# Stores one tile behind, weight transposes held back, and a split first and last tile in a fused attention and FFN training kernel

## The chip, the cores and the metric

The kernel runs on one core of a Trainium2 chip. The metric is the device time of one execution in microseconds; before the change the median of four runs was 837.86 us (839.8, 839.36, 836.18, 836.36). Engine names follow the profile: PE is TensorE, PEld its weight loads, DVE VectorE, ACT ScalarE, POOL GpSimd and SP SyncE. SP does nothing but issue transfers; ACT and POOL issue some as well, and a "queue" is the list of transfers that one engine issues in order.

## What is computed

The reference is the forward pass and all the gradients of one transformer block, with S = 2048 rows, width D = 640, FFN width F = 1728, 32 heads of 20, in bf16:

```python
def _A_ref(x, wqkv, wo):                       # linear attention
    q, k, v = split_heads(x @ wqkv)            # 32 heads x 20
    phi = lambda t: jnp.where(t > 0, t + 1, jnp.exp(t)) + 1e-6
    pq, pk = phi(q), phi(k)
    kv  = einsum("bhsd,bhse->bhde", pk, v)
    z   = einsum("bhsd->bhd", pk)
    num = einsum("bhqd,bhde->bhqe", pq, kv)
    den = einsum("bhqd,bhd->bhq", pq, z)[..., None] + 1e-6
    return merge_heads(num / den) @ wo
def _B_ref(x, w_gate, w_up, w_down):
    return (silu(x @ w_gate) * (x @ w_up)) @ w_down

h  = x + _A_ref(layernorm(x), wqkv, wo)
h2 = h + _B_ref(layernorm(h), w_gate, w_up, w_down)
outputs: h2, and for a given grad_out the gradients of x, wqkv, wo, w_gate, w_up, w_down
```

## The kernel before

The 2048 rows are 16 row tiles of 128 (ST = 16); 640 columns are five blocks of 128 (DT = 5) and, for the accumulators in PSUM, two halves of 320 columns (NCH); F is 14 blocks of 128, the last one not full (FT = 14). One matmul therefore is mostly 128 x 128 weights by 320 columns. `mm_row` (its matmul is line 118) writes both halves of one accumulator. Accumulators come from a pool of four, row tiles of work from pools of five and later seven (`wk`), big tensors from a pool of five (`big`), strips from a pool of four.

The stages, in the order of time, with the rows of before.py:

- *Layer norm 1 and the projections* (8 to 58 us, lines 181 to 288). `load_x` brings row tiles of x, `wqk` holds the k and q columns of wqkv, loaded in a K half (line 186) and a Q half (line 188), all on SP's queue except tile 1, which ACT issues. `ln1_stats(t)` takes mean and variance (lines 124, 125) and from them rstd (129, 130); for the first two tiles a part of this is on DVE and the last step on POOL. `ln1(t)` normalises into xn (line 238, DVE), transposes five blocks on PE (242), and copies them out on ACT as xnT (243). `kq_mm(t, 0)` and `kq_mm(t, 1)` are the two projections, with phi on ACT (251, 252) and DVE (257, 259). In this part the program order on PE, DVE and ACT is the written order: stats of tile 0, stats of tile 1, xn of tile 0, and so on.
- *z, Y, KVT and the normalisation* (58 to about 100 us). The sum of phi(k) over the rows is formed as zs and zl (297, 298) and spread as zb (386). `KVT`, one half of the strip `yk`, is filled with zeros (379) before masked blocks are written into it (400). `normalise` divides the phi(q) tiles (366 to 373). W2 is KVT by wo.
- *h1 and layer norm 2* (100 to about 152 us, lines 413 to 438). At tile t the residual is added (422) and stored; two tiles behind (u = t - 2) hn is formed (437). In five of these steps a block of W2 is transposed by SP into a `stg` buffer and written by POOL to the DRAM scratch scr_W2T (435). rstd of this layer norm runs on POOL too.
- *FFN forward and backward in four column groups* (152 to 460 us), ending in scratch copies: the columns needed for dhn, and the w_down gradient transposed, scr_dwdT.
- *The dh1 loop* (460 to 614 us, lines 592 to 638). At tile t, PE computes dhn from `cols` (54 matmuls a tile), `ln_bwd` ends in dh (143), SP transposes it into dh1T (603). Three tiles behind (LAG_C = 3, u = t - 3) PE multiplies dh1T by W2T into ps_dp, and DVE forms dq through pr, S1 and nS1. Besides, POOL loads the row tile pqr (606), DVE multiplies it into pqs_tm (623), and for the first 14 tiles SP transposes one block of the w_down gradient, dwd (609), which POOL stores to the output (611). Before the last tile's dp, three blocks of GT = dh1^T pqs_tm are accumulated over the first 15 row tiles (`gt_part`, 587), and their last row tile comes after.
- *GT, dKVT, dz and WV2* (614 to 631 us, lines 645 to 703). SP transposes wqkv in 15 pieces into wqkvT (`tr_mat`, `tr_piece`, 566). ACT issues the load of all x rows again as xn_r (`act_load`, 148), which DVE normalises (690). GT and dKVT are stored to scratch by POOL (667, 677). WV2 is copied by ACT (699) and transposed by SP as wvk (700).
- *The wqkv gradient and dxn* (630 to 765 us): per row tile, SP transposes pk, dq and dk into a ring of tiles (717, 718, 750), and PE multiplies them by wqkvT and wvk (767). xnT is read back in four parts by ACT.
- *The output* (765 to 834 us, lines 805 to 826): per row tile 28 matmuls of the FFN's activations by w_down (815), the add of h1 (818), a store by POOL (819). The last tile has its two halves in two accumulators, with an add (822) and a store (823) for each, by ACT and by SP.

What sets the order: `tc.manual_schedule(engines=...)` keeps the written order on the engines named; in the dh1 loop and after only on SP (then SP and DVE). On the others a scheduler orders the program by its own estimate of when operands are ready, so that a line that stands later can be issued earlier. `tc.issue_after(i)` puts what it encloses behind the instruction i on the same engine; it adds no wait. A written order holds inside its block: the 15 transposes of wqkvT stand in the code behind the whole dh1 loop, in the next block, and yet twelve of them are issued on SP between the transposes dh1T of the last two tiles.

Of the kernel before, what the change touches and what calls it, by code (L numbers as in the profile page):

```python
# [10 lines left out]
ALU = mybir.AluOpType  # L11
# [4 lines left out]
P = 128  # L16
# [4 lines left out]
def kernel(  # L21
# [161 lines left out]

    load_x(nc.sync, 0, 1)
    load_x(nc.scalar, 1, 2)
    nc.sync.dma_start(out=wqk[:, :, D:2 * D], in_=A_wqkv[:, D:2 * D].rearrange("(k p) n -> p k n", p=P))
# [50 lines left out]
    def ln1(t):  # L237
        nc.vector.tensor_scalar(out=xn[:, t, :], in0=x_tm[t // 8][:, t % 8, :], scalar1=mv1[:, t, 0:1],
                                scalar2=rstd1[:, t:t + 1], op0=ALU.subtract, op1=ALU.mult)
        tp = psum.tile([P, D], BF16, name="ps_t", tag="mm")  # L240
        for kt in range(DT):
            nc.tensor.transpose(tp[:, kt * P:(kt + 1) * P], xn[:, t, kt * P:(kt + 1) * P], ident[:])
        nc.scalar.copy(out=xnT[:, t], in_=tp[:].rearrange("p (k c) -> p k c", c=P))  # L243

# [21 lines left out]
    with tc.manual_schedule(engines={EngineType.PE, EngineType.DVE, EngineType.Activation}):  # L266
# [4 lines left out]
        ln1_stats(0)  # L271
        ln1_stats(1)
        ln1(0)
# [101 lines left out]
    with tc.manual_schedule(engines={EngineType.PE, EngineType.DVE}):  # L375
        yk = strips.tile([P, 2, DT, D], BF16, name="yk", tag="S")
        Yt = yk[:, 0]
        KVT = yk[:, 1]
        nc.vector.memset(KVT, 0.0)
        for i in range(DT):  # L380
# [35 lines left out]
        for t in range(ST + 2):  # L416
# [151 lines left out]

    def tr_mat(dst, src):
        for i in range(DT):  # L570
            tr_piece(dst, src, i)

    with tc.manual_schedule(engines={EngineType.SP}):
# [4 lines left out]
        pqs_tm = big.tile([P, ST, D], BF16, name="pqs_tm", tag="B")  # L578
        pqr = {}
        dh1Ts = {}  # L580

# [10 lines left out]
        for t in range(ST + LAG_C):  # L592
            if t < ST:
                if t % 2 == 0 and 2 < t + 2 < ST:
                    load_cols(t // 2 + 1)
                cols = colp[t // 2]
                ps = mm("ps_dhn")
                mm_row(ps, lambda k: cols[:, t % 2, k, :],
# [3 lines left out]
                dh1Ts[t] = dh1T[:].rearrange("p (k c) -> p k c", c=P)  # L602
                nc.sync.dma_start_transpose(out=dh1Ts[t], in_=dh1[:, t, :])
# [19 lines left out]
            nc.vector.tensor_tensor(out=hb(pqs_tm[:, u, :]), in0=hb(pq[:]), in1=bc(rall[:, u, :]), op=ALU.mult)  # L623
            dp = wk("dp")
# [15 lines left out]
    with tc.manual_schedule(engines={EngineType.SP, EngineType.DVE}):  # L640
# [13 lines left out]
        for k in (2, 0, 1):  # L654
            tr_mat(wqkvT[:, 5 * k:5 * k + 5, :], A_wqkv[:, k * D:(k + 1) * D])
        act_load(xn_r[:], x_v)

        GT = mat("GT")
        for i in range(DT):
            ps = gts.pop(i, None)  # L660
            if ps is None:
                ps = mm("ps_gt")
                gt_part(ps, i, 0, ST)
            else:
                gt_part(ps, i, ST - 1, ST)
            nc.scalar.copy(out=half(GT[:, i, :]), in_=row(ps))
# [138 lines left out]
        for t in range(ST):  # L805
# [5 lines left out]
            ps = mm("ps_o")  # L811
            pss = [ps, ps] if t < ST - 1 else [ps, mm("ps_o2")]
            for ci, (n0, n1) in enumerate(NCH):
                for j in range(FT):
                    nc.tensor.matmul(pss[ci][:, ci, :320], lhsT=mT[:, t % 4, j, :], rhs=wd[:, j, n0:n1],  # L815
                                     start=(j == 0), stop=(j == FT - 1))
            if t < ST - 1:
                nc.vector.tensor_tensor(out=half(h1r[:]), in0=row(ps), in1=half(h1r[:]), op=ALU.add)  # L818
                nc.gpsimd.dma_start(out=o0_v[:, t, :], in_=h1r[:])
            else:  # L820
                for ci, (n0, n1) in enumerate(NCH):
                    nc.vector.tensor_tensor(out=h1r[:, n0:n1], in0=pss[ci][:, ci, :320], in1=h1r[:, n0:n1], op=ALU.add)
                    (nc.scalar, nc.sync)[ci].dma_start(out=o0_v[:, t, n0:n1], in_=h1r[:, n0:n1])
            if t < DT:
# [34 lines left out]
```

## Time and profile before

One execution was profiled; every number below is of that one.

| | us |
|---|---|
| time of the profiled execution | 839.06 |
| its span (first to last instruction) | 837.1 |
| median of four runs | 837.86 |
| PE busy | 825.4 (99%) |
| DVE busy | 444.0 (53%) |
| ACT busy | 291.6 (35%) |
| POOL busy | 190.2 (23%) |
| granted clock of PE, mean | 0.998 |

A row of a timeline has the start, the duration, the engine, the line in before.py, the operation and its operands as out<-in, how many equal instructions the row holds (x10), and in brackets the idle time of the engine before it and what ended it. A row "SPq" or "ACTq" is the issuing of transfers, not the transfers. A row of the waits says which engine waited at which line for which engine or transfer: total us, times, longest. "Landing" is the time from the start of the issue to the arrival of the data. Row tiles are counted from 0, so the last is tile 15.

### The profile page before, as it was taken

The page shows a single profiled execution, that of the slowest core. Times are in us where ns is not written, and L with a number is a line of the kernel's source. Part 1 is how long each engine was busy: PE and PEld are TensorE (multiplying, and loading weights), DVE is VectorE, ACT ScalarE, POOL GpSimd, SP SyncE. Part 2 cuts the span into 40 slices and gives each one's busy share as a digit, 9 for nine tenths or more (in the row PEclk, how much of TensorE's full clock was granted, in tenths as well). Part 3 has the DMA queues.
Part 4 walks back from the last instruction along what each step waited for, and adds up shares of the span by engine and source line. Part 5 has one row for each costly group of instructions (what it writes and reads, how often), then busy time and mean ns, then how long its engine had stood idle before and what let it go on. Part 6 is the DMA issues. An engine that isn't in the chain of part 4 may idle for free.

```text
span 837.1 us, 13990 instructions
## 1 busy us (share of the span) xinstructions
PE 825.4 (99%) x5509; PEld 528.3 (63%) x5509; DVE 444.0 (53%) x872; ACT 291.6 (35%) x414; POOL 190.2 (23%) x347
## 2 busy tenths in 40 slices
PE   8999999999999999999999999999999999999998
PEld 6666656555555555555656777777666677777776
DVE  7979757791086028700940155797854266621121
ACT  6983422770184035401920232322222133331101
POOL 2330133222412312231225012111101122111322
PEclk9999999999999999999999999999999999999999
DMA  9995889998668988992686769656579988899962
GB/s 295 207 328 137 170 164 251 261 220 208 160 138 215 209 185 187 208 231 70 148 236 172 249 172 246 168 113 153 115 216 224 152 145 176 165 199 215 271 181 95
DMA packets 282785, 160.17 MB, mean 191 GB/s; under 512 B 238128, under 2 KB 269408, under 8 KB 282720
## 3 DMA queue, kind: packets, MB, share of 16 engines
q1 hardware_dynamic: 253472, 80.71, 51.0%
q0 software_dynamic: 17968, 65.55, 25.4%
q10 hardware_dynamic: 11280, 13.03, 5.8%
q8 instruction: 43, 0.70, 0.4%
q14 instruction: 22, 0.18, 0.1%
HBM read 47.43 MB, written 55.10 MB: 122 GB/s over the span
## 4 chain that ended last, share of the span: by engine, by line
PE 87%; DVE 6%; DMA 3%; SPq 2%; ACT 1%; issue 1%; POOL 0%; DVEq 0%; ACTq 0%; POOLq 0%
PE ps_dw L533 20%; PE ps_dhn L118 14%; PE ps_dxn L767 8%; PE ps_o L815 7%; PE pg L465 6%; PE pu L470 5%; PE ps_dwqk L118 5%; PE ps_dm L309 4%; PE ps_kq L118 3%; PE ps_y L118 3%; PE ps_dk L118 2%; PE ps_dp L118 2%; PE pdm L309 2%; PE ps_a L118 2%; PE ps_gt L587 1%; DMA ring<-dk 1%
## 5 line engine op out<-in xcount | busy, mean ns | idle before, releaser
L118 PE MATMUL ps_dhn<-wgT,cols 128*128 128x320 bf16 x864 | 119.5, 299 | 0.0
L533 PE MATMUL ps_dw<-dd,hn 128*128 128x448 bf16 (+1 forms) x640 | 118.8, 346 | 0.0
L118 PEld LDWEIGHTS <-cols 128*128 128x128 bf16 x864 | 84.5, 98 | 32.9
L533 PEld LDWEIGHTS <-hn 128*128 128x128 bf16 x640 | 62.6, 98 | 54.2
L535 DVE CAST dwev<-ps_dw 128x896 bf16<-128x896 f32 (+3 forms) x12 | 10.9, 908 | 124.1 <-PE ps_dw L533 124.1
L502 POOL DMA_DIRECT2D scr_dT<-stg x64 | 34.7, 543 | 168.6 <-DMA stg<-dd 166.1
L535 ACT CAST dwev<-ps_dw 128x896 bf16<-128x896 f32 (+1 forms) x20 | 17.6, 879 | 158.0 <-PE ps_dw L533 158.0
L465 PE MATMUL pg<-wgu,hnT 128*128 128x448 bf16 (+1 forms) x320 | 63.6, 346 | 0.0
L470 PE MATMUL pu<-wgu,hnT 128*128 128x448 bf16 (+1 forms) x320 | 63.6, 346 | 0.0
L815 PE MATMUL ps_o<-wd,mT 128*128 128x320 bf16 x448 | 62.6, 299 | 0.0
L767 PEld LDWEIGHTS <-ring 128*128 128x128 bf16 x480 | 47.5, 99 | 21.5 <-DMA ring<-dk 2.3
L533 PE MATMUL ps_dw<-m_s,dh 128*128 128x448 bf16 (+1 forms) x320 | 60.5, 346 | 0.3 <-DVE m_s L497 0.3
L815 PEld LDWEIGHTS <-mT 128*128 128x128 bf16 x448 | 43.8, 98 | 17.0
L767 PE MATMUL ps_dxn<-wqkvT,ring 128*128 128x320 bf16 x320 | 52.6, 304 | 2.0 <-DMA ring<-dk 2.0
L533 PEld LDWEIGHTS <-dh 128*128 128x128 bf16 x320 | 31.3, 98 | 27.5 <-issue 0.5
L470 PEld LDWEIGHTS <-hnT 128*128 128x128 bf16 x320 | 31.3, 98 | 27.1
L465 PEld LDWEIGHTS <-hnT 128*128 128x128 bf16 x320 | 31.3, 98 | 27.1
L309 PEld LDWEIGHTS <-dh2T 128*128 128x128 bf16 x320 | 31.3, 98 | 25.1
L118 PE MATMUL ps_kq<-wqk,xnT 128*128 128x320 bf16 x320 | 46.1, 299 | 0.8 <-ACT xnT L243 0.8
L309 PE MATMUL ps_dm<-wdT,dh2T 128*128 128x448 bf16 (+1 forms) x240 | 46.9, 344 | 0.0
L818 DVE TENSOR_TENSOR h1r<-ps_o,h1r 128x640 bf16<-128x640 f32 x15 | 12.4, 825 | 56.6 <-PE ps_o L815 36.8
L118 PEld LDWEIGHTS <-xn_r 128*128 128x128 bf16 x320 | 30.7, 98 | 13.4 <-DVE xn_r L690 1.6
(159 smaller groups left out, 1288.3 us busy)
## 6 DMA issues: line engine op xcount, KB each, us to landing
cols<-scr_dT POOLq DMA_DIRECT2D x7, 1728.0 KB, 8.5
scr_dT<-stg POOLq DMA_DIRECT2D x48, 224.0 KB, 3.2
scr_m<-m_s POOLq DMA_DIRECT2D x12, 448.0 KB, 5.0
out_dram<-dwev POOLq DMA_DIRECT2D x30, 112.0 KB, 2.1
scr_dT<-stg POOLq DMA_DIRECT2D x16, 192.0 KB, 3.2
scr_xnT<-xnT SPq DMA_DIRECT2D x4, 640.0 KB, 6.0
scr_pk<-pk SPq DMA_DIRECT2D x4, 640.0 KB, 6.7
scr_pq<-pqa SPq DMA_DIRECT2D x4, 640.0 KB, 7.9
```

The lines of the kernel that those rows point to most:

```text
L118: nc.tensor.matmul(ps[:, ci, :320], lhsT=lhs(k), rhs=rhs(k, n0, n1), start=(start and k == 0), stop=(stop and k == n - 1))
L309: nc.tensor.matmul(ps[:, c, :w], lhsT=dh2T[:, kt, (t + c) * P:(t + c + 1) * P], rhs=wdT[:, kt, o:o + w], start=(kt == 0), stop=(kt == DT - 1))
L465: nc.tensor.matmul(pg[:, c, :w], lhsT=hnT[:, kt, (t + c) * P:(t + c + 1) * P], rhs=wg[:, kt, 0:w], start=(kt == 0), stop=(kt == DT - 1))
L470: nc.tensor.matmul(pu[:, c, :w], lhsT=hnT[:, kt, (t + c) * P:(t + c + 1) * P], rhs=wg[:, kt, w:2 * w], start=(kt == 0), stop=(kt == DT - 1))
L502: nc.gpsimd.dma_start(out=scr_dT[t + c, :, KO[g]:KO[g] + GK[g], :], in_=stg[:, :GK[g], :])
L533: nc.tensor.matmul(ps[:, c, :w], lhsT=lhs(t), rhs=rhs(t), start=(t == 0), stop=(t == ST - 1))
L535: copy(out=ev[:, :len(parts), :w], in_=ps[:, :len(parts), :w])
L587: nc.tensor.matmul(ps[:, ci, :320], lhsT=dh1[:, t, i * P:(i + 1) * P], rhs=pqs_tm[:, t, n0:n1], start=(t == 0), stop=(t == ST - 1))
L767: nc.tensor.matmul(ps[:, ci, :320], lhsT=lhs[:, i, :], rhs=rhs[:, i, n0:n1], start=(k == 0 and i == 0), stop=(k == 2 and i == DT - 1))
L815: nc.tensor.matmul(pss[ci][:, ci, :320], lhsT=mT[:, t % 4, j, :], rhs=wd[:, j, n0:n1], start=(j == 0), stop=(j == FT - 1))
L818: nc.vector.tensor_tensor(out=half(h1r[:]), in0=row(ps), in1=half(h1r[:]), op=ALU.add)
```

## The change

- The load of x tile 0 is split in two halves of 320 columns, one by SP and one by ACT; tile 1 moves from ACT to SP, behind the first half. The statistics of tile 1 move from before xn of tile 0 to behind it. The copy of the first xnT is shared: blocks 0 to 2 by ACT, blocks 3 and 4 by DVE.
- The fill of KVT with zeros is put behind the subtraction that makes zl, on DVE. (In the program before, the scheduled place was in the middle of layer norm 1, at 26.84 us.)
- The store of a W2T block is written one tile later than its transpose.
- The transpose of a w_down gradient block goes ahead of the tile's dh1T on SP, and its store one tile later. The multiply into pqs_tm goes one tile earlier, right behind the load of pqr.
- The 15 transposes of wqkvT are put behind the last dh1T. The three parts of GT before the last dp stop two row tiles earlier (13 instead of 15 row tiles); the two tiles come after.
- The last output tile is computed in pieces of 320, 192 and 128 columns, each with its own add and store, by ACT, POOL and SP.

```diff
-    load_x(nc.sync, 0, 1)
-    load_x(nc.scalar, 1, 2)
+    nc.sync.dma_start(out=x_tm[0][:, 0, 0:320], in_=x_v[:, 0, 0:320])
+    nc.scalar.dma_start(out=x_tm[0][:, 0, 320:640], in_=x_v[:, 0, 320:640])
+    load_x(nc.sync, 1, 2)
...
-        nc.scalar.copy(out=xnT[:, t], in_=tp[:].rearrange("p (k c) -> p k c", c=P))
+        tpv = tp[:].rearrange("p (k c) -> p k c", c=P)
+        if t == 0:
+            ln1_stats(1)
+            nc.scalar.copy(out=xnT[:, t, 0:3], in_=tpv[:, 0:3])
+            nc.vector.tensor_copy(out=xnT[:, t, 3:5], in_=tpv[:, 3:5])
+        else:
+            nc.scalar.copy(out=xnT[:, t], in_=tpv)
...
         ln1_stats(0)
-        ln1_stats(1)
         ln1(0)
...
-        nc.vector.tensor_tensor(out=half(zs[1][:]), in0=row(ps), in1=half(zs[0][:]), op=ALU.subtract)
+        last_zs = nc.vector.tensor_tensor(out=half(zs[1][:]), in0=row(ps), in1=half(zs[0][:]), op=ALU.subtract).ins
...
-        nc.vector.memset(KVT, 0.0)
+        with tc.issue_after(last_zs):
+            nc.vector.memset(KVT, 0.0)
...
+            if 2 <= u <= DT + 1:
+                nc.gpsimd.dma_start(out=mat_v(scr_W2T)[:, :, (u - 2) * P:(u - 1) * P], in_=w2t)
             if 1 <= u <= DT:
                 w2t = stage()[:, :DT, :]
                 nc.sync.dma_start_transpose(out=w2t, in_=W2[:, u - 1, :])
-                nc.gpsimd.dma_start(out=mat_v(scr_W2T)[:, :, (u - 1) * P:u * P], in_=w2t)
...
+                if t < FT:
+                    dwds[t] = wk("dwd", pool=1)
+                    nc.sync.dma_start_transpose(out=dwds[t][:].unsqueeze(1), in_=scr_dwdT[:, t * P:(t + 1) * P])
...
-                nc.sync.dma_start_transpose(out=dh1Ts[t], in_=dh1[:, t, :])
-            if t - LAG_C + 1 in range(ST):
-                pqr[t - LAG_C + 1] = wk("pqr", pool=1)
-                nc.gpsimd.dma_start(out=pqr[t - LAG_C + 1][:], in_=scr_pq_v[:, t - LAG_C + 1, :])
-            if t < FT:
-                dwd = wk("dwd", pool=1)
-                nc.sync.dma_start_transpose(out=dwd[:].unsqueeze(1), in_=scr_dwdT[:, t * P:(t + 1) * P])
-                rows = min(P, F - t * P)
-                nc.gpsimd.dma_start(out=out_6[t * P:t * P + rows, :], in_=dwd[:rows, :])
+                last_dh1T = nc.sync.dma_start_transpose(out=dh1Ts[t], in_=dh1[:, t, :]).ins
+            u = t - LAG_C + 1
+            if u in range(ST):
+                pqr[u] = wk("pqr", pool=1)
+                nc.gpsimd.dma_start(out=pqr[u][:], in_=scr_pq_v[:, u, :])
+                nc.vector.tensor_tensor(out=hb(pqs_tm[:, u, :]), in0=hb(pqr[u][:]), in1=bc(rall[:, u, :]), op=ALU.mult)
+            if 0 < t <= FT:
+                dwd = dwds.pop(t - 1)
+                r0 = (t - 1) * P
+                nc.gpsimd.dma_start(out=out_6[r0:min(r0 + P, F), :], in_=dwd[:min(P, F - r0), :])
...
-                    gt_part(gts[i], i, 0, ST - 1)
+                    gt_part(gts[i], i, 0, ST - 3)
...
-            nc.vector.tensor_tensor(out=hb(pqs_tm[:, u, :]), in0=hb(pq[:]), in1=bc(rall[:, u, :]), op=ALU.mult)
...
-            tr_mat(wqkvT[:, 5 * k:5 * k + 5, :], A_wqkv[:, k * D:(k + 1) * D])
+            for i in range(DT):
+                with tc.issue_after(last_dh1T):
+                    tr_piece(wqkvT[:, 5 * k:5 * k + 5, :], A_wqkv[:, k * D:(k + 1) * D], i)
...
-                gt_part(ps, i, ST - 1, ST)
+                gt_part(ps, i, ST - 3, ST)
...
-            pss = [ps, ps] if t < ST - 1 else [ps, mm("ps_o2")]
-            for ci, (n0, n1) in enumerate(NCH):
+            chs = NCH if t < ST - 1 else [(0, 320), (320, 512), (512, 640)]
+            for ci, (n0, n1) in enumerate(chs):
+                if ci and t == ST - 1:
+                    ps = mm("ps_o2")
+                po = ps[:, ci % 2, :n1 - n0]
...
+                if t == ST - 1:
+                    nc.vector.tensor_tensor(out=h1r[:, n0:n1], in0=po, in1=h1r[:, n0:n1], op=ALU.add)
+                    (nc.scalar, nc.gpsimd, nc.sync)[ci].dma_start(out=o0_v[:, t, n0:n1], in_=h1r[:, n0:n1])
```

More of the change, by code (lines that the diff above doesn't have):

```diff
@@ L567, in tr_piece @@
                                     in_=src[i * P:(i + 1) * P, ks[0] * P:(ks[-1] + 1) * P])
-    def tr_mat(dst, src):
-        for i in range(DT):
-            tr_piece(dst, src, i)
     with tc.manual_schedule(engines={EngineType.SP}):
@@ L579 @@
         pqr = {}
+        dwds = {}
         dh1Ts = {}
@@ L811 @@
             ps = mm("ps_o")
-            pss = [ps, ps] if t < ST - 1 else [ps, mm("ps_o2")]
-            for ci, (n0, n1) in enumerate(NCH):
+            chs = NCH if t < ST - 1 else [(0, 320), (320, 512), (512, 640)]
[3 more added lines that the diff above has]
+                po = ps[:, ci % 2, :n1 - n0]
                 for j in range(FT):
-                    nc.tensor.matmul(pss[ci][:, ci, :320], lhsT=mT[:, t % 4, j, :], rhs=wd[:, j, n0:n1],
+                    nc.tensor.matmul(po, lhsT=mT[:, t % 4, j, :], rhs=wd[:, j, n0:n1],
                                      start=(j == 0), stop=(j == FT - 1))
+                if t == ST - 1:
+                    nc.vector.tensor_tensor(out=h1r[:, n0:n1], in0=po, in1=h1r[:, n0:n1], op=ALU.add)
+                    (nc.scalar, nc.gpsimd, nc.sync)[ci].dma_start(out=o0_v[:, t, n0:n1], in_=h1r[:, n0:n1])
             if t < ST - 1:
@@ L819 @@
                 nc.gpsimd.dma_start(out=o0_v[:, t, :], in_=h1r[:])
[L820 to L823, printed above, removed]
             if t < DT:
```

## The prediction

> **What bounds the kernel now.** I read the page first, then the chain of waits on PE (TensorE), then the timeline where PE waits, then stretches of equal length around the late waits.
>
> ```profile
> span 837.1 us, 13990 instructions
> PE 825.4 (99%) x5509; PEld 528.3 (63%) x5509; DVE 444.0 (53%) x872; ACT 291.6 (35%) x414; POOL 190.2 (23%) x347
> ```
>
> PE is busy for 99% of the span. An edit can win only in the 11.7 us that are left, or where PE is busy at a lower clock. The waits say which of these the edits meet (columns: total us, times, longest):
>
> ```profile
> PE ps_dxn L767 <- DMA ring<-dk: 2.0, 1, 2.0
> ...
> PE ps_t L242 <- DVE xn L238: 1.6, 2, 0.9
> ...
> PE ps_dp L118 <- DMA dh1T<-dh: 1.3, 1, 1.3
> ...
> PE ps_a L118 <- DVE xr L422: 0.7, 1, 0.7
> ```
>
> The timeline (start, us, engine, what) shows the places:
>
> ```profile
> 5.15 0.88 DVE L124 BATCH_NORM_STATS2 st<-x_tm 128x6 f32<-128x320 bf16 x2
> 5.31 0.57 POOL L130 TENSOR_TENSOR rstd<-lnv,nhalf 128x1 f32<-128x1 f32 x1 [3.95 <-DVE lnv L129]
> ...
> 6.37 0.44 DVE L238 TENSOR_SCALAR xn<-x_tm,mv,rstd 128x640 bf16<-128x640 bf16 x1
> ...
> 9.75 1.52 PE L118 MATMUL ps_kq<-wqk,xnT 128*128 128x320 bf16 x10
> ```
>
> ```profile
> 26.84 1.39 DVE L379 MEMSET yk<- 128x1600 uint32 x1 [0.28 <-DVE st L124]
> 30.33 0.45 PE L242 MATMUL ps_t<-ident,xn 128*128 128x128 bf16 x5 [0.85 <-DVE xn L238]
> ```
>
> ```profile
> 592.22 17.19 SPq L566 DMA_TRANSPOSE wqkvT<-in_A_wqkv_dram  x12
> ...
> 601.99 8.90 PE L587 MATMUL ps_gt<-pqs_tm,dh 128*128 128x320 bf16 x63 [0.30 <-DVE pqs_tm L623]
> ...
> 609.52 1.21 SPq L603 DMA_TRANSPOSE dh1T<-dh  x1
> ...
> 612.16 1.53 PE L118 MATMUL ps_dp<-W2T,dh1T 128*128 128x320 bf16 x10 [1.27 <-DMA dh1T<-dh]
> ```
>
> ```profile
> 661.75 2.82 PE L767 MATMUL ps_dxn<-wqkvT,ring 128*128 128x320 bf16 x10 [2.00 <-DMA ring<-dk]
> ```
>
> So: the first tile waits on a chain of small steps, a fill of 1.39 us on DVE makes PE late once, twelve weight transposes stand ahead of the last dh1T on SP's queue, and PE waits for a transposed ring tile at 661.75.
>
> **The change part by part**, as gains against the profiled execution.
>
> *First tile.* The statistics of tile 1 (from 5.15) hold xn(0) back to 6.37, though its rstd is ready at 5.31 + 0.57 = 5.88: 0.49 us can go. Sharing the copy of xnT (0.69 us, ACT) between ACT and DVE saves at most about 0.25. But the second projection also needs the Q half of wqk. Its load is issued at 2.31 and lands 7.2 later, at 9.5; the projection began at 9.75, so 0.25 is the most there. Tile 1 now goes ahead of both weight halves on SP: one issue (0.44) more in front, and 80 KB more on that ring, 0.2 us at the page's early 300 to 400 GB/s. A stall of 0.2 us at tile 1's transposes should go as well. I take 0.3; the ends are a loss of 0.2 (Q half later) and a gain of 0.75 (Q half no limit).
>
> *Fill of KVT.* PE's wait at 30.33 is 0.85 us, 1.18 in the row of its weight load; I take 1.0 of these ends. The fill goes behind the last use of zs (59.48 + 0.82 = 60.3), where DVE then sits idle for 4.22 us until zb, so 1.39 us is covered. Without that cover it would cost up to 1.39 in the normalisation.
>
> *W2T stores a tile later.* POOL runs the rstd of the LN behind these five stores, and PE waits 0.7 us for it once. In the program as built the order on every queue stays the same, so I take 0; the upper end is 0.7. The lower end is 0 too, as no instruction goes ahead of another that was before it.
>
> *w_down gradient.* On SP a dwd transpose (median 1.26 us) goes ahead of each dh1T; the store goes a tile later on POOL, where 103.0 us of waiting for dwd end; pqs_tm goes a tile earlier on DVE. From 460 to 593 us PE has no wait:
>
> ```profile
> 460.00:593.00 133.00, 133.00 (x981) 95.79 (x980) 86.47 (x184) 36.19 (x58) 20.76 (x37) 1.00 0.65 178
> ```
>
> (stretch, sum, then busy us of PE, weight loads, DVE, ACT, POOL, then clock, DMA share, GB/s). Nothing can be won there: 0. The cover is the lag of three tiles, 3 x 8.7 us, less dh1T's longest landing of 8.5: 17 us. Without it each of the 14 tiles could lose 1.2 us. Behind that sits one new wait: a dwd buffer comes free a tile later, so on SP a dh1T can wait for POOL's store of an earlier dwd; the store itself has waited for nothing by then, as its tile landed a tile before (landing 10.0 at the longest).
>
> *wqkvT behind the last dh1T, gt parts shortened.* dh(15) is ready at 598.07 + 0.48 = 598.55, and its transpose waits until 609.52 behind weight transposes. Put first, it lands before 609 even at its longest 8.5 us. PE then loses neither the 1.27 nor the 0.30 (pqs_tm comes a tile earlier, and the gt parts stop two tiles sooner): 1.57 by PE's rows, 2.1 by those of its weight loads; I take 1.9. The 12 gt matmuls taken out ahead of dp(15) come back behind it (12 x 0.136).
> What this makes late: 15 transposes now run from about 600 to 619.5 rather than 12 by 609.4 and 3 more by 614.7, so four more of them run beside the 2.6 MB xn_r load (issued 614.03, landing 11.3 later, needed by DVE at 628.61). Twelve took 17.19 us at a DMA share of 0.6, so each is 0.86 us of the engines, four 3.4.
>
> ```profile
> 606.00:610.00 4.00, 4.00 (x32) 2.90 (x30) 4.00 (x10) 0.00 (x0) 0.00 (x0) 1.00 0.58 121
> ...
> 618.00:622.00 4.00, 4.00 (x32) 2.86 (x31) 2.31 (x3) 0.69 (x1) 0.00 (x0) 1.00 1.07 356
> 622.00:626.00 4.00, 3.92 (x64) 3.14 (x64) 1.17 (x5) 0.69 (x1) 1.01 (x2) 1.00 0.39 134
> 626.00:630.00 4.00, 4.00 (x43) 2.75 (x32) 3.45 (x7) 2.51 (x4) 0.76 (x1) 1.00 0.96 340
> ```
>
> The idle share of 622 to 626 takes 0.61 x 4 = 2.4 of the 3.4. From 626 to 662 the DMA is full nearly throughout, so the remaining 1.0 reaches ring<-dk, and the stall at 661.75 grows by 1.0. Net 1.9 - 1.0 = 0.9. Good end: the chain comes as early as PE does, 2.1. Bad end: the transposes starve beside the big load as the slowest wqkvT did (landing 6.3 for 2.9), 3.4 more: 1.9 - 4.4, a loss of 2.5.
> After that stall 15 matmuls run at half pace: 10 take 2.82 us for 1.52, 5 more 1.27 for 0.84, together 1.7 us. I leave these as they are. [...]
>
> *Last tile in thirds.* PE: 14 x (0.082 + 0.056) for 14 x 0.136, 0.03 more (192 columns in proportion). The last add, 0.49 at 320 columns and 0.82 at 640, is about 0.29 at 128: 0.20 less. The last store lands 1.6 after its issue as before. Gain 0.15. But the middle third, added by 833.6, goes out through POOL, where stores of h1r land 2.1 (median) to 3.5 later: 835.7 is hidden before 836.1, 837.1 would cost 1.0. I take the median. [...]
>
> **Sum.** 0.3 + 1.0 + 0 + 0 + 0.9 + 0.15 = 2.35 us. The profiled execution took 839.06 (span 837.1 and 2.0 around it), 1.2 above the median 837.86 of the four runs (two near 839.6, two near 836.3). 839.06 becomes 836.7; against the median I predict 835.5.
>
> **Rivals.**
> 1. *The ring keeps up with PE.* Nothing of wqkvT or xn_r is left by 626, and the chain moves with PE: 2.35 + 1.0 = 3.35, 834.5. For it: the idle share at 622 to 626. Against: 3.4 does not fit in 2.4.
> 2. *The slow stretch goes.* If ring<-dk comes 2 us nearer, the wait and the 1.7 us of slow clock go as well: 3.35 + 2.0 + 1.7 = 7.05, 830.8. For it: fewer pieces would have to compete after 626. Against: nothing of the work after 626 is removed.
> 3. *Slower: transposes against the xn_r load.* If ring<-dk lands more than 3.35 us late against PE, all gains are spent. At the bad end (4.4) it is 1.05 slower, 838.9, and if the slow stretch doubles, 840.6. For it: the slowest wqkvT landed 6.3 us after issue beside that load, and the SP row of one ring<-scr_pk takes 5.59. Against: xn_r can begin 2 us earlier.
> 4. *The head does nothing*, as wqk's Q half lands later: 835.5 + 0.5 = 836.0.
>
> **How the numbers follow.** Forecast 0.45, rival 1 0.20, rival 2 0.08, rival 3 0.12, rival 4 0.15. A change of 0.5%, 4.2 us, is about what a measurement of this kernel can tell from none. Faster by more: rival 2 and the upper tails of the forecast and rival 1 (a median may lie 1.7 us off, as the two pairs show): 0.22. Slower by more: no mechanism but the far end of rival 3, widened by the same 1.7: 0.09. Within: 0.69. The range runs from 832.6 (rival 1 and the pairs' spread) to 838.8 (rival 3).
>
> **What would show it.** dh1T(15) issued just behind dh(15) and no wait of ps_dp; no wait of ps_t at 29 us, and the fill inside the idle time before tzs; the second projection near 9.5; the stall before ps_dxn at 3 us (right), 2 (rival 1), none (rival 2), or above 5 (rival 3), with PEclk beside it; the last store landing 0.15 earlier. A new wait of PE between 460 and 593, or on W2T, would make the prediction wrong.

## The result, and the profile after

The changed kernel is slower by a little: the ratio to the kernel before is 1.0024, with a 95% interval of 1.0013 to 1.0036, that is 2.0 us (1.1 to 3.0). The medians are 838.26 us of 46 executions (834.63 to 846.98) and 836.42 of 70 (834.14 to 842.51). I had forecast 2.35 us faster. The ratios here and below come with the measurements and are not the quotients of the medians beside them; executions over 1.5% above the fastest of their kernel (none of these 116, a few further down) are left out of them.

The profile seems to say the opposite. The profiled execution of the changed kernel took 835.26 us, 3.8 less than that of before (839.06). Both are single draws from wide distributions: that of before lies 2.6 above its median, that of after 3.0 below its own. The page of the changed kernel begins:

```profile
span 833.2 us, 14022 instructions
PE 822.4 (99%) x5523; PEld 529.2 (64%) x5523; DVE 444.1 (53%) x874; ACT 290.3 (35%) x414; POOL 190.8 (23%) x348
```

Its chain of waits on PE (columns: total us, times, longest) no longer has ps_t, ps_dp, ps_gt or ps_dxn. In their place the head waits for the weights:

```profile
PE ps_kq L118 <- DMA wqk<-in_A_wqkv_dram: 2.5, 2, 1.4
...
PE ps_a L118 <- DVE xr L429: 0.7, 1, 0.7
```

In the timeline (start, us, what, idle time before it and its releaser) the head shows that everything in front came earlier, as planned, and that PE then stood twice before a half of wqk. The second projection starts at 10.61, where it was 9.75:

```profile
4.99 0.45 DVE L239 TENSOR_SCALAR xn<-x_tm,mv,rstd 128x640 bf16<-128x640 bf16 x1 [0.69 <-POOL rstd L130]
...
7.46 1.52 PE L118 MATMUL ps_kq<-wqk,xnT 128*128 128x320 bf16 x10 [1.13 <-DMA wqk<-in_A_wqkv_dram]
...
10.61 1.53 PE L118 MATMUL ps_kq<-wqk,xnT 128*128 128x320 bf16 x10 [1.36 <-DMA wqk<-in_A_wqkv_dram]
```

The fill stands where it was meant to, and DVE still waits for zb behind it:

```profile
60.07 1.39 DVE L386 MEMSET yk<- 128x1600 uint32 x1 [0.28 <-issue]
64.01 1.49 DVE L372 TENSOR_TENSOR tzs<-pqa,zb 128x2560 bf16<-128x2560 bf16 x1 [2.55 <-ACT zb L393]
```

Around the last dh1T, PE runs through; ps_dp starts at 607.97 without a wait, and the 15 wqkvT transposes take SP until 624.7:

```profile
597.37 10.76 PE L592 MATMUL ps_gt<-pqs_tm,dh 128*128 128x320 bf16 x78
599.88 24.84 SPq L574 DMA_TRANSPOSE wqkvT<-in_A_wqkv_dram  x15
607.97 1.52 PE L118 MATMUL ps_dp<-W2T,dh1T 128*128 128x320 bf16 x10
...
612.83 0.38 ACTq L148 DMA_DIRECT2D xn_r<-in_A_x_dram  x1
```

And the end of the program, in the kernel before:

```profile
831.20 0.54 POOL L803 DMA_DIRECT2D out_dram<-dwv  x1
833.98 0.49 DVE L822 TENSOR_TENSOR h1r<-ps_o,h1r 128x320 bf16<-128x320 f32 x1 [1.35 <-PE ps_o L815]
```

and in the changed kernel:

```profile
827.29 0.54 POOL L832 DMA_DIRECT2D out_dram<-h1r  x1 [2.14 <-DVE h1r L831]
827.42 0.29 DVE L831 TENSOR_TENSOR h1r<-ps_o,h1r 128x128 bf16<-128x128 f32 x1 [0.42 <-PE ps_o L828]
827.74 0.36 SPq L832 DMA_DIRECT2D out_dram<-h1r  x1
```

The last add starts at 827.42, and the span ends at 833.19, 5.77 later. Before it was 833.98 to 837.10, 3.12. The queue records show the difference: POOL closes with a long DRAIN (columns: how many, then the shortest, middle and longest in ns, then the first and last start):

```profile
L854 POOLq DRAIN  x3: 46/93/5047, 831.2 to 836.8; - x3
```

```profile
L866 POOLq DRAIN  x3: 46/97/5127, 827.3 to 832.9; - x3
```

In the kernel before the long one runs from 831.18 to 836.23, beside the last tile's work, and SP closes its own queue at 836.34. In the changed kernel it runs from 827.27 to 832.40; SP has closed at 829.6, and nothing else runs from then on. The rest of the span, 0.8 us, has only short DRAIN and semaphore instructions (0.14 us at the longest), as before from 836.34 on.

To see what each part did, I took from every profile the starts of a few PE instructions, and subtracted stage by stage. Each column is one execution of the changed kernel (the last four are single runs, of which more below), each number the change of that stage against the profile of before (us). The stages: to the fifth tile's first projection; from there to ps_z (the fill lies here); to ps_wv (the last dh1T); to the first ps_dxn; to the 61st ps_dxn matmul (the ring's stall); from there to the last add; from the last add to the end.

| stage | after, 1st profile | `a_look1` | `a_look2` | `a_look3` | `a_look4` |
|---|---|---|---|---|---|
| head | +0.64 | +3.62 | +1.55 | +0.53 | +0.90 |
| to ps_z | -1.17 | -1.17 | -1.17 | -1.16 | -1.17 |
| ps_z to ps_wv | -2.22 | -2.17 | -1.52 | -2.14 | -2.12 |
| ps_wv to ps_dxn | 0.00 | 0.00 | 0.00 | +3.34 | 0.00 |
| first ps_dxn | -3.85 | -3.84 | -3.61 | -3.85 | +1.61 |
| to the last add | +0.03 | +0.03 | +0.03 | +0.03 | +0.03 |
| end | +2.64 | +2.64 | +2.64 | +2.64 | +2.64 |
| time, us | 835.26 | 838.31 | 837.12 | 838.60 | 841.09 |

Three rows are nearly the same in all five: the fill (-1.17), the last dh1T (about -2.2; in `a_look2` ps_a waited 0.7 longer at 120 us) and the end (+2.64). Two change from execution to execution: the head, and the stretch from the wqkvT transposes to the ring.

### The profile page after: what moved, and what is told of

The parts are those of the page before. It is cut to its first block, busy times and chain, and to the rows that moved or that the text cites. A ratio compares the mean times of both kernels' runs of the same rounds, so it can differ in the third digit from the quotient of the medians.

```text
span 833.2 us, 14022 instructions
## 1 busy us (share of the span) xinstructions
PE 822.4 (99%) x5523; PEld 529.2 (64%) x5523; DVE 444.1 (53%) x874; ACT 290.3 (35%) x414; POOL 190.8 (23%) x348
## 4 chain that ended last, share of the span: by engine, by line
PE 93%; DVE 3%; DMA 1%; issue 1%; SPq 0%; ACT 0%; POOL 0%; POOLq 0%; DVEq 0%; ACTq 0%
PE ps_dw L541 21%; PE ps_dhn L118 14%; PE ps_dxn L777 8%; PE ps_o L828 7%; PE pg L473 6%; PE pu L478 5%; PE ps_dwqk L118 5%; PE ps_kq L118 5%; PE ps_dm L315 5%; PE ps_y L118 3%; PE ps_gt L592 3%; PE ps_dk L118 3%; PE ps_dp L118 3%; PE ps_a L118 2%; PE pdm L315 2%; DMA wqk<-in_A_wqkv_dram 1%
## 5 line engine op out<-in xcount | busy, mean ns | idle before, releaser
L828 PE MATMUL ps_o<-wd,mT 128*128 128x320 bf16 (+2 forms) x462 | 62.7, 295 | 0.0
L777 PEld LDWEIGHTS <-ring 128*128 128x128 bf16 x480 | 47.0, 98 | 18.2
L828 PEld LDWEIGHTS <-mT 128*128 128x128 bf16 x462 | 44.5, 98 | 16.6
L834 DVE TENSOR_TENSOR h1r<-ps_o,h1r 128x640 bf16<-128x640 f32 x15 | 12.3, 824 | 56.7 <-PE ps_o L828 29.1
L118 PEld LDWEIGHTS <-xnT 128*128 128x128 bf16 x320 | 30.6, 98 | 13.7 <-DMA wqk<-in_A_wqkv_dram 1.5
```

Source lines behind the costliest of these rows:

```text
L118: nc.tensor.matmul(ps[:, ci, :320], lhsT=lhs(k), rhs=rhs(k, n0, n1), start=(start and k == 0), stop=(stop and k == n - 1))
L777: nc.tensor.matmul(ps[:, ci, :320], lhsT=lhs[:, i, :], rhs=rhs[:, i, n0:n1], start=(k == 0 and i == 0), stop=(k == 2 and i == DT - 1))
L828: nc.tensor.matmul(po, lhsT=mT[:, t % 4, j, :], rhs=wd[:, j, n0:n1], start=(j == 0), stop=(j == FT - 1))
```

## The experiments

The theories: **T**, the tail costs 2.6 us through POOL's drain; **H**, the head costs, since the weights come later; **R**, later sharpened to **C** and **C'**, the transfers between 600 and 660 us starve one another and the held transposes make this worse. All ratios are against the kernel before, in runs on the same chip; where there is a single execution, there is a time and no ratio.

### The tail alone, undone and done

`a_oldtail` is the changed kernel with the tail of before. `b_tail` is the kernel before with

```diff
-            for ci, (n0, n1) in enumerate(NCH):
+            chs = NCH if t < ST - 1 else [(0, 320), (320, 512), (512, 640)]
...
+                    (nc.scalar, nc.gpsimd, nc.sync)[ci].dma_start(out=o0_v[:, t, n0:n1], in_=h1r[:, n0:n1])
```

> The changed kernel with the last tile in two halves again (ACT and SP queues), everything else as changed. Theory T (the tail costs): in the profile after, POOL's closing drain starts behind the last store that POOL issued and lasts 5.1 us in both kernels (before: 831.18 to 836.23, hidden; after: 827.27 to 832.40, and nothing else runs from 829.6 on). From the last add to the end of the span it was 3.1 us before and is 5.8 after. So this run should be 2.65 us shorter than the changed kernel: ratio to before 0.999 instead of 1.0024. Rival R (the ring stage costs, in the executions that were not profiled): the tail is worth its planned 0.15 us and the ratio stays at 1.002 to 1.003.

> The kernel before with the last tile in thirds alone (ACT, POOL, SP queues). Theory T: 2.65 us longer than before, ratio 1.003, and a profile with the drain of POOL as the last thing, about 5 us from the last POOL store to its end. Rival R: the predicted gain of 0.15 us, ratio 1.000.

`a_oldtail`: 836.9 us, ratio 1.0003 (0.9974 to 1.0032). `b_tail`: 841.05, ratio 1.0041 (1.0010 to 1.0071), so thirds alone make the kernel slower. The ratios are too wide to measure 2.6 us, but the profiles do: the last add to the end takes 3.06 us with the old tail and 5.77 with thirds on the kernel before. In the timeline of `a_oldtail` POOL's last store of h1r (828.24) is that of the tile before, and its last issue of all (828.90, a part of a weight gradient) is 2.8 us older than the last add (831.68):

```profile
828.24 0.54 POOL L829 DMA_DIRECT2D out_dram<-h1r  x1 [2.92 <-DVE h1r L828]
828.90 0.54 POOL L813 DMA_DIRECT2D out_dram<-dwv  x1
```

Later, `best` moved the middle third from POOL to ACT, with thirds otherwise as they were: last add 844.75, end 847.75, 3.00. The three other profiles with the thirds on ACT and SP have 3.00 as well. So in these runs it is the queue, not the thirds. The thirds are worth 0.12 us in the end stage, less the 0.03 that PE takes longer. Theory T holds. More of the thirds stays hidden: in `best` SP has closed at 846.68, but POOL's drain, behind the tile before (POOL's last issue is at 841.94), runs to 846.96 and ends last again.

### The head as before

`a_oldhead` is the changed kernel with

```diff
-    nc.sync.dma_start(out=x_tm[0][:, 0, 0:320], in_=x_v[:, 0, 0:320])
-    nc.scalar.dma_start(out=x_tm[0][:, 0, 320:640], in_=x_v[:, 0, 320:640])
-    load_x(nc.sync, 1, 2)
+    load_x(nc.sync, 0, 1)
+    load_x(nc.scalar, 1, 2)
...
+        ln1_stats(1)
         ln1(0)
...
```

and with the whole copy of the first xnT on ACT again.

> The changed kernel with the first tile's loads, statistics and copy as before. In the profile after, PE waited twice for the halves of wqk (1.13 and 1.36 us) and the second projection began at 10.61 instead of 9.75. Theory H (the head costs): the edit is worth a loss of about 0.5 us at 119 us once the 1.0 of the fill is taken out, so this run is 0.5 us shorter than the changed kernel, ratio 1.0018; the second projection begins at 9.7 again. Rival: wqk's landing varies from execution to execution and is the cause of the wide spread of the changed kernel (834.6 to 847.0): then the spread shrinks to that of before, and the ratio falls by more, to about 1.000.

The time is 841.33, ratio 1.0029 (0.9998 to 1.0061): it tells nothing of half a microsecond. In the profile the second projection is back at 9.69 and the fifth tile at 20.55 instead of 21.25. The spread did not shrink (835.64 to 849.54), so the rival, that wqk's landing is the cause of all of the spread, falls. Over all the profiles of this study the fifth tile's first projection starts at 21.9 us on average with the new head (nine executions, 21.05 to 24.23) and at 20.8 with the old one (nine, 20.40 to 21.90). So the head costs 1.1 us on average, more than its 0.6 in the first profile (the middle ones of the nine, 21.8 and 20.6, say the same). The reason is in the landings: the K half of wqk landed at 7.21 to 8.38 us with the new head, at 6.08 to 7.33 with the old one. Three of the nine with the new head (`a_oldhold`, mean clock 0.54 from 8 to 11.5 us; `a_look1`, 0.50 from 9.15 to 15.98; `a_look2`, 0.997 over the execution) and one of the nine with the old one (`b_late`, 0.998 over the execution) also have a stretch of half clock in this stage.

### The transposes free again, and held alone

`a_oldhold` is the changed kernel with

```diff
-                with tc.issue_after(last_dh1T):
-                    tr_piece(wqkvT[:, 5 * k:5 * k + 5, :], A_wqkv[:, k * D:(k + 1) * D], i)
+                tr_piece(wqkvT[:, 5 * k:5 * k + 5, :], A_wqkv[:, k * D:(k + 1) * D], i)
...
-                    gt_part(gts[i], i, 0, ST - 3)
+                    gt_part(gts[i], i, 0, ST - 1)
...
```

and `b_hold` is the kernel before with the opposite edit; there the multiply into pqs_tm stays a tile later.

> The changed kernel with the wqkvT transposes free to go ahead of the last dh1T again and the gt parts over 15 row tiles. Rival R (the ring stage costs): held back, the transposes make ring<-dk late in many executions, with a stall and a slow clock behind it. Then this run has the narrower spread of before, and its median lies no higher than the changed kernel's although PE loses the 2.25 us ahead of dKVT: ratio 1.000 to 1.0024, with the wait of ps_dp back. If the ring stage costs nothing on average, it is 2.25 us longer than the changed kernel: ratio 1.005.

> The kernel before with the wqkvT transposes behind the last dh1T and the gt parts two row tiles shorter, alone. PE reaches ps_wv 1.9 to 2.3 us earlier. Theory C: of this the ring takes back most in the usual execution, since ring<-dk lands when the bulk loads allow it: the stall before ps_dxn is 3.5 to 4.5 us instead of 2.0, and the ratio is 0.998 to 1.000. If the ring moves with PE, the stall stays 2.0 and the ratio is 0.9975.

`a_oldhold`: 839.99, ratio 1.0026 (1.0001 to 1.0050). `b_hold`: 839.67, ratio 1.0023 (0.9995 to 1.0050). In `a_oldhold` the wait of ps_dp is back (2.6 us) with one of ps_gt for pqs_tm (1.4), and in this execution (842.11) the stage to ps_wv is 6.3 us longer than in the changed kernel's first profile, a slow clock included (mean clock of the execution 0.994). The time does not decide between the two expectations: it lies just above the range of the one, and the other (1.005) is the end of the interval. For `b_hold` 1.0023 lies above both expectations, though the interval reaches 1.000; in its profile PE comes to ps_wv only 0.6 us earlier, not 1.9 to 2.3. The part that was to give PE 2.2 us gives nothing in the median. Its profiled execution (843.58) shows where the time goes; the ring's stall, of which I had spoken, is not there, but an earlier one is:

```profile
PE ps_dk L118 <- DMA wvk<-wvk: 3.4, 2, 3.0
PE ps_dk L118 <- ACT dwqk L713: 1.9, 1, 1.9
```

The slowest wqkvT landed 17.0 us after its issue (6.3 before), xn_r after 14.0 (11.3 before). The transposes of wvk stand behind wqkvT on SP, and PE waits for them. Behind these waits the granted clock is at half for 6.8 us (from 648.9 on; 10 matmuls take 2.83 us there, 1.52 at 659.52).

### The last xnT_r loads later

`b_late` is the kernel before with one edit:

```diff
-        for c in range(4):
+        def load_xnT(c):
             act_load(xnT_r[:, 4 * c:4 * c + 4], scr_xnT[4 * c:4 * c + 4].rearrange("t p k c -> p t k c"))
+
+        load_xnT(0)
+        load_xnT(1)
...
+            if t in (3, 6):
+                load_xnT(1 + t // 3)
```

> The kernel before with one thing changed: the last two of the four xnT_r loads are issued by ACT in the ring loop (about 655 and 675 us) instead of at 638 to 640. In the profiles so far ring tiles landed 13 to 16 us after issue whenever the last xnT_r load landed 13 to 15 us late (before, and four of the variants), with the stall before ps_dxn of 2.0 to 3.5 us and a slow clock behind it; in the profile of the changed kernel that load landed after 7.1 and there was no stall. Theory C (the bulk loads starve the ring): here the ring tiles land within 8 us, the stall and the slow stretch go, 3.85 us in the profile; the median 1 to 4 us below before, ratio 0.995 to 0.999. Rival Q (the ring waits for SP's own order or for dk, the loads only happen to be there): stall as before, ratio 1.000.

The time is 836.34, ratio 0.9977 (0.9956 to 0.9999). In the profile ps_dxn starts at once; for comparison, in the kernel before PE had 2.00 us of waiting in this place and 10 matmuls in 2.82 us:

```profile
659.93 0.84 PE L772 MATMUL ps_dxn<-wvk,ring 128*128 128x320 bf16 x5
660.61 1.52 PE L772 MATMUL ps_dxn<-wqkvT,ring 128*128 128x320 bf16 x10
```

The ring tiles issued between 630 and 663 us landed after 3.5 / 5.4 / 6.2 us (least, median, most); before it was

```profile
DMA to landing us min/median/max: 3.1/8.4/16.1
```

One profile without a stall could be chance, since the changed kernel's first one has none either; the other profiles settle it. Of the fifteen with the four loads together, seven have the stall (1.6 to 5.3 us), and in these seven the last xnT_r load took 13.6 to 18.2 us. Of the eight without it, six have 5.7 to 9.8 us, and two (`a_oldhold` and `a_hold10`) 12.8 and 14.1. The three with the last loads late have 5.7 to 6.0 us, ring tiles within 6.2 us and no such stall (two of them wait 0.7 us for another ring tile). So in these profiles the stall before ps_dxn goes with the plain loads of xnT_r that are in flight beside the ring's transposes, and goes away with them; SP's order and dk, which `b_late` does not change, do not make it by themselves. Theory C holds for this place; what it is worth on average is known only roughly (0.1 to 3.7 us, by the interval).

### Head and tail put right, with 15 and with 10 transposes held

`best` is the changed kernel with the head of before and the middle third on ACT's queue. `best_late` adds the late xnT_r loads. `a_hold10` is the changed kernel with this edit alone, which lets SP do five transposes in the time in which it otherwise waits for dh(15):

```diff
             for i in range(DT):
+                if k == 2:
+                    tr_piece(wqkvT[:, 5 * k:5 * k + 5, :], A_wqkv[:, k * D:(k + 1) * D], i)
+                    continue
                 with tc.issue_after(last_dh1T):
```

`best10` and `best10_late` are `best` and `best_late` with the same edit. The first two ran beside one set of runs of the kernel before, the three with 10 held beside another, on another chip.

> The changed kernel with two parts changed back or replaced: the head as before, and the middle third of the last tile on ACT's queue instead of POOL's. Theory T: POOL's drain begins with the last store of the tile before (near 831 less what is won), so the span ends about 3 us after the last add, 2.6 less than in the changed kernel. With the head's 0.7 that is 3.3 us less: ratio to before 0.9985 from 1.0024. What it still has of the changed kernel is the fill and the transposes held back. If thirds cost by themselves, whatever the queue, the end stays 5.8 us behind the last add.

> The run before this one (head as before, middle third on ACT) with the last two xnT_r loads late as well. Theory C: the 3.3 us won ahead of the ring are kept, since nothing starves it: 839.06 - 1.1 (fill) - 2.25 (held transposes) - 3.85 (stall and slow clock) = 832 in the profile, ratio about 0.993, and a narrower spread. Rival Q: the stall grows by the 3.3 us that PE comes earlier, ratio 0.9985 or above.

> The changed kernel with only the last 10 of the 15 transposes held behind the last dh1T; the first five go where SP otherwise waits for dh(15). PE's gain ahead of ps_wv stays (2.25 us), and the transposes end about 613 us instead of 622 to 630, as early as in the kernel before. Theory C': the collision with xn_r is cut to two or three pieces, the spread narrows to that of before, and the median falls by 2 to 3 us against the changed kernel's: ratio 0.998 to 1.000 (the tail's 2.64 and the head's 0.7 are still in). Rival W: spread and median as in the changed kernel.

> Head as before, middle third on ACT's queue, 10 transposes held. Theory C': against the run before this one 2.64 + 0.7 us less, ratio 0.994 to 0.996. The ring's stall may stand, as the xnT_r loads are where they were.

> The same with the last two xnT_r loads late. Theory C' and theory C together: both collisions gone, best execution as in the run with 15 held (831.8), but without its slow executions near 842; median 832 to 833, ratio 0.993 to 0.995. If slow executions near 842 remain in the same share, holding fewer transposes does not remove the collision.

| kernel | median us | lowest to highest | ratio to before (95%) |
|---|---|---|---|
| best (15 held) | 836.81 | 833.29 to 849.71 | 0.9976 (0.9944 to 1.0008) |
| best_late (15 held) | 833.30 | 831.75 to 842.92 | 0.9967 (0.9934 to 1.0001) |
| a_hold10 | 836.85 | 835.39 to 841.32 | 0.9991 (0.9970 to 1.0011) |
| best10 | 833.83 | 830.90 to 838.81 | 0.9950 (0.9930 to 0.9970) |
| best10_late | 832.45 | 831.53 to 833.66 | 0.9928 (0.9907 to 0.9950) |

With 15 held, `best_late` has nine executions between 831.7 and 835.4 and three near 842; with 10 held, none of six is above 833.7. The profile of `best_late` fell on one of the three (842.41) and shows what happens in them, in the chain of waits, in the tile view of xn_r, and in the stretches (PE, weight loads, DVE, ACT, POOL, clock, DMA share, GB/s):

```profile
PE ps_dwqk L118 <- DVE xn_r L694: 6.1, 1, 6.1
```

```profile
DMA to landing us min/median/max: 20.7/20.7/20.7
```

```profile
624.00:628.00 4.00, 3.89 (x29) 2.57 (x27) 1.90 (x3) 3.24 (x5) 0.03 (x1) 1.00 1.11 306
628.00:632.00 4.00, 0.00 (x0) 0.00 (x0) 0.00 (x0) 0.72 (x2) 0.00 (x0) 0.80 1.05 405
632.00:636.00 4.00, 1.98 (x6) 0.62 (x6) 2.49 (x7) 0.00 (x0) 0.00 (x0) 0.50 1.54 203
```

The xn_r load, 11.3 us in both first profiles, took 20.7 here; PE stands still from 628 to 632 at a DMA share of 1.05 and 405 GB/s, and when it goes on its clock is at half (0.50 from 632 to 636). That is a loss of 6.3 us in one stage and 2.9 in the next.

In the eighteen profiles the slowest of the wqkvT transposes landed later with transposes held, and mostly this load too. With none held (four), the slowest wqkvT took 5.3 to 7.0 us and xn_r 10.8 to 11.3; with 15 held (eleven), 9.0 to 19.9 and 11.3 to 20.7. With 10 held (three), it is 10.3 to 12.5 and 12.3 to 14.3, no better than with 15; but the pieces are issued earlier, and the last wqkvT has landed by 624.4, where with 15 held it was 629.1 to 643.2.

The profiled execution of `best` (849.71) is the slowest that was profiled, and it loses in the same stretch, against the profile of before: 1.0 us ahead of ps_dwqk, 8.2 ahead of ps_dxn and 3.1 at the ring, with a slowest wqkvT of 19.9 us. All executions together: of the kernels with 15 transposes held (the changed one in two sets of runs, and five others), 29 of 118 executions took over 7 us more than the fastest of their set (without the five longest of these, still 24 of 113); of the six variants with 10 or none held, 4 of 66; of the kernel before, in its four sets, 12 of 169. This is counted over different kernels, so it is a strong hint and not a measurement of one edit. `a_hold10` against the changed kernel beside it, `a_again` below, has the same sign, 2 of 12 above 840 us for 4 of 12. Half of its expectation failed, though: its median is 0.4 us below that of `a_again`, not 2 to 3.

### The changed kernel again

> The changed kernel once more, for a second profile and beside the others. Theory C' (in a share of the executions the 15 held transposes, the xn_r load and the two stores starve one another): in the slow runs of kernels with held transposes so far, xn_r landed 13.5 to 20.7 us after issue (11.3 in the fast profile) and the last wqkvT at 635 to 643 (629.6 in the fast one), and PE waited 3 to 8 us more before ps_dwqk or ps_dk. So this run is again wide, 834.5 to 846, median 837.5 to 840; if its profile falls on a slow execution, the loss stands between 625 and 660 us, with a landing of xn_r above 12 or of the last wqkvT after 632. Rival W (the wide spread comes from the head or the FFN part): a slow profile shows its loss before 600 us.

`a_again` took 837.25 in the median (834.84 to 849.47), ratio 0.9991 (0.9960 to 1.0023); its profile, 835.84, shows none of the later stalls, so it could not tell theory C' from theory W (that the spread comes from the head or the FFN). Its interval includes no change and reaches almost to the 0.24% of the larger sample. Four single executions followed:

> The changed kernel, a look for a wide execution. Theory C': if it takes over 838 us, the loss against the first profile of the changed kernel lies between 620 and 675 us and a landing of xn_r over 12 us or of the last ring tiles over 12 us stands beside it. Theory W: the loss lies before 600 us.

> As the look before it: over 838 us by theory C' with the loss between 620 and 675 us, by theory W before 600 us; near 835.5 it tells nothing of either.

> As the two looks before it: over 838 us by theory C' with the loss between 620 and 675 us, by theory W before 600 us; near 835.5 it tells nothing of either.

> As the three looks before it: over 838 us by theory C' with the loss between 620 and 675 us, by theory W before 600 us; near 835.5 it tells nothing of either.

The table of stages above has the four. Both theories are right in part. In `a_look1` (838.31) the loss of 3 us is in the head. PE waited 1.93 us for the K half, and the clock was at half behind it for 6.8 us:

```profile
8.19 1.93 PE L118 MATMUL ps_kq<-wqk,xnT 128*128 128x320 bf16 x10 [1.93 <-DMA wqk<-in_A_wqkv_dram]
...
11.35 2.85 PE L118 MATMUL ps_kq<-wqk,xnT 128*128 128x320 bf16 x10 [0.69 <-DMA wqk<-in_A_wqkv_dram]
```

```profile
5.74:9.15 3.41, 1.48 (x17) 1.13 (x15) 1.83 (x7) 0.48 (x1) 0.56 (x1) 1.00 1.06 368
9.15:15.98 6.83, 6.14 (x31) 3.79 (x29) 3.90 (x12) 3.63 (x6) 1.83 (x4) 0.50 1.07 363
```

In `a_look3` (838.60) ps_dk waited 3.2 us for ACT to copy out an accumulator; ACT was issuing the xnT_r loads until 645.2. In `a_look4` (841.09) the ring's stall was back, at twice its length before:

```profile
661.36 2.82 PE L777 MATMUL ps_dxn<-wqkvT,ring 128*128 128x320 bf16 x10 [3.99 <-DMA ring<-dk]
```

with ring tiles landing up to 17.5 us after issue and an xnT_r load after 16.6. None of the four shows the 6 to 12 us losses of `best` and `best_late`; for the changed kernel's own executions above 842 us it stays open which place they lose in.

## Why the prediction was wrong

*First tile.* Predicted a gain of 0.3, with ends of -0.2 and +0.75; it is a loss of 1.1 us on average, and 3.6 in the worst profile. The step that failed is "the second projection also needs the Q half": I let only the Q half limit, and made it too little late. Both halves stand one issue further back on SP and landed 1.1 us later in the first profile (K at 7.41 for 6.31, Q at 10.57 for 9.48), where I had counted 0.44 for the issue and 0.2 for the bytes. And the K half held up the first projection as well (1.13 us in the first profile, 1.93 in `a_look1`). Besides, a wait of about 2 us in this place was followed by the slow clock in two profiles of the changed kernel (1.93 us in `a_look1`, 2.3 in `a_look2`), for which I had no term.

*Fill.* Predicted 1.0 of 0.85 to 1.18; every kernel that has the edit gains 1.17. The cover named is where it was said to be.

*W2T stores and w_down gradient.* Predicted 0 and 0. PE's wait at ps_a stays at 0.7 us in the first profile (over all of them 0.5 to 1.6 with the edit, 0.6 to 1.4 without), and from the first ps_dhn to the last the changed kernel and that of before agree within 0.01 us.

*wqkvT and gt parts, the gross gain.* Predicted 1.9; the two profiles differ by 2.25 at this place. Kernels without the edit differ among themselves here (`b_late` and `b_tail` are 0.3 and 0.5 us shorter than the profile of before), so the gain is 1.8 to 2.3. Held alone, in `b_hold`, it is 0.74, and ps_gt waited 0.8 us for pqs_tm, which comes a tile later there: the two edits belong together, which the prediction said only in a half sentence.

*wqkvT, what it makes late.* The first half was right: more transposes beside the xn_r load, and with 15 held the slowest of them landed after 9.0 to 19.9 us (5.3 to 7.0 with none held), the load after 11.3 to 20.7 (10.8 to 11.3). That the delay reaches the ring holds in a part of them only: with 15 held and the xnT_r loads as they were, the stall before ps_dxn is there in four of ten profiles (2.3 to 5.3 us), with none held in two of three (2.0). The size was wrong too. I had the transposes end at 619.5, and SP was at them until 624.7; and I added up engine time (3.4 less 2.4, 1.0 us) as if the work stood in one line. The runs show transposes and plain loads that land late together, after 13 to 20 us, in a part of the executions and not in others: from nothing (both profiles near 835.5) to 5.5 us (`a_look4`), and to 12 in relatives with the same held transposes. Rival 2 describes the executions without a stall and without the slow clock, rival 3 the others. I had given each a chance as if the kernel were one or the other; it is a mixture.

*Last tile.* Predicted a gain of 0.15, a loss of 1.0 at most; it is a loss of 2.64 in every profile. The step that failed is "the middle third, added by 833.6, goes out through POOL": it prices the store's landing (1.83 in the profile after, better than the 2.1 assumed), and leaves out POOL's closing drain. It was in the trace of before, 5.05 us long and hidden by 0.1 us only (it ended at 836.23, SP closed at 836.34). It started there at 831.18, with POOL's last issue (831.20); my estimate from these numbers is that an issue over 0.1 us later would already have shown.

*The base.* I subtracted from the one profile and carried its 2.0 + 1.7 us at the ring over as a fixed part. The median of 70 executions of before is 836.42, 2.6 less than that profile's time, so a usual execution cannot have had all of it.

The sum in place of mine: head +1.1, fill -1.2, last dh1T -2.2, tail +2.6, together +0.3 us, the same for each execution but for the head's spread. The remaining 1.7 of the measured 2.0 (0.8 to 2.7 by the interval) must come from the stretch of 600 to 675 us, by difference, if the other stages are as in the profiles; what its average is, in the kernel before and after, no run here measures directly. Against my terms the tail is off by 2.8 us and the head by 1.4, together 4.2 of the 4.35 between forecast and result; the other terms nearly cancel.

On the clock: half clock followed waits of 1.93 (`a_look1`), 2.00 (before) and 3.99 us (`a_look4`), and ten matmuls took 2.82 to 2.85 us there for 1.52. It did not follow waits of 2.26 (`a_oldtail`, at the ring), 3.18 (`a_look3`) and 3.54 us (`a_oldhead`, at the ring); the ten matmuls behind these took 1.52 or 1.53. So in these runs the length of the wait alone does not decide; what does, no run shows. Before, the clock is at half from 661.82 to 665.23, 3.41 us; PE was busy for 1.42 of the 3.41 us ahead of that, and in `a_look1` for 1.48. The 15 matmuls in this stretch took 2.82 and 1.27 us for 1.52 and 0.84, which is the 1.7 us at the ring before.

## What to carry to other kernels

Before an edit is costed by one profile, see where that profile lies among the timed executions; where it is in the upper part, its stalls are partly chance, and a gain of their size is not to be had. Transfers that are moved later must be weighed against every bulk load that is in flight there: releasing only as many transposes as the queue could do in its idle time (5 ahead, 10 behind) kept PE's gain (2.26 us from the last ps_dhn to ps_wv, in all three profiles), and of the 30 executions with it only one took over 7 us more than the fastest of its kernel, 7.9. At the end of this program the queue of a last store cost more than the store: POOL's cost 2.64 us, ACT's (`best`) nothing that shows. Look at what each engine does after its last transfer.

The version that this points to, `best10_late` (fill moved, 10 transposes behind the last dh1T, shorter gt parts, head as before, thirds by ACT and SP, the last two xnT_r loads late), ran at 0.9928 of the kernel before (0.9907 to 0.9950), in six executions from 831.53 to 833.66 us.

## What the runs showed of the hardware

- POOL's closing drain took 5.05 us before (831.18 to 836.23) and 5.13 in the changed kernel (827.27 to 832.40). In both it started within 0.02 us of POOL's last issue (831.20 and 827.29), and in the changed kernel that last store had landed 1.83 us after its issue.
- A plain load of 2.6 MB beside transposes of another queue (xn_r) landed after 11.3 (before) to 20.7 us (`best_late`) in one and the same place, and single transposes of wqkvT after 2.8 (after) to 19.9 (`best`); from 620 to 636 us in `best_late` the DMA share was 1.05 to 1.54.
- The granted clock was at half for 3.41 us before (from 661.82) and for 6.83 us in `a_look1` (from 9.15), behind waits of PE of 2.00 and 1.93 us; behind waits of 3.18 (`a_look3`) and 3.54 us (`a_oldhead`) ten matmuls took 1.52 and 1.53 us, as at full clock.
- The last third's store (SP, 32 KB in rows of 256 bytes) landed 1.55 us after its issue; SP's last store in the kernel before (80 KB in rows of 640 bytes) landed after 1.63.
